# Where the causal mask is added in a segment-recurrent attention kernel: a matmul of the identity, or an add on VectorE

## The chip, the cores and the metric

The kernel runs on one core of a Trainium2 chip. The metric is the device time of one execution in microseconds (us). Engines go by their short names: PE is TensorE's matmul stream, PEld its weight loads, DVE is VectorE, ACT is ScalarE, POOL is GpSimd, SP is the engine that issues most of the DMAs. PSUM is the memory that PE writes its sums into; DVE and ACT read them from there.

## What is computed

Two pairs of layers run one after the other over a sequence of 2048 tokens of width 448. Layer A is attention with 16 heads of 256, in segments of 32 tokens; each segment attends to 8 memory rows and to itself, and its first 8 output rows are the memory of the next segment. Layer B is a gated feed-forward. The part of the reference that matters:

```
def _A_ref(x, mem0, Wq, Wk, Wv, Wo, seg_len):
    ...
    L = M + seg_len
    idx = jnp.arange(L)
    mask = (idx[:, None] < M) | (idx[:, None] >= idx[None, :])
    mem = mem0
    for s in range(n_seg):
        h = jnp.concatenate([mem, xs], axis=1)
        ...
        scores = jnp.einsum('bhqe,bhke->bhqk', q, k) * scale
        scores = jnp.where(mask[None, None], scores, -1000000000.0)
        p = _softmax(scores, axis=-1)
        ...
        mem = o[:, :M, :].copy()
...
x = x + _A_ref(_layernorm(x, axis=-1), ...)
x = x + _B_ref(_layernorm(x, axis=-1), ...)
x = x + _A_ref(_layernorm(x, axis=-1), ...)
x = x + _B_ref(_layernorm(x, axis=-1), ...)
```

## The kernel before, in words

At the start (until 93.6 us, where the first matmul of a step stands) the weights of query and key, and of value and output, are multiplied into one matrix per head pair (`A_sb`, `B_sb`). Then 69 steps follow, `for g in range(nsteps + 1)`. Step g works on segment g of the first attention layer and, four steps later, on segment g-4 of the second one; the code calls these two the chains. `active(g)` gives the chains of a step: only the first for g = 0 to 3, both for g = 4 to 63, only the second for g = 64 to 67. So there are 60 **two-layer steps**, 30 with even g and 30 with odd g. Odd steps also carry the feed-forward (`Feed`: `gate_up` and `down`), which gives PE more to do.

The 16 heads are in two halves, hf = 0 and 1 (8 heads times 16 rows are 128 partitions). In a step, in the order in which `step` issues it:

- `project` (L383) multiplies the tokens by `A_sb`, seven groups for each half; the results go from PSUM to the tiles `TQ` and `TZ`.
- `scores_m` (L458) makes the scores `Sm` of the 8 memory rows of both chains and calls `weights_of` (L412), the softmax on DVE and ACT: `mx` (L415, largest of a row), `se` (L417, subtract it), Exp on ACT (L418), `ssum` (L420), `rs` (L422, reciprocal), for the memory rows `rs` times `blk` (L424), and the product into `PM` or `PX` (L425).
- `flipped` (L427) transposes `PM` on PE into the PSUM tile `pps`, and DVE copies it to `PT` (L432).
- `scores_x` (L466) makes the scores `Sx` of the segment rows, a tile of 128 x 4 x 40 in one PSUM tile. In the kernel before, the first matmul is the identity times `maskS` (128 x 160 numbers, 0 or -1e6, built once at the start), which puts the mask there; 16 matmuls of 40 columns are then added to it.
- `weigh_m` (L479) multiplies the tokens by `PT`: two matmuls into `ya`, three into `yb`. DVE copies `ya` to `Y` (L485), ACT copies `yb` to `Y` (L490).
- `project_out` (L522) multiplies `Y` by `B_sb` into `ox`, the largest piece of PE's work; `weigh_x` and `finish` follow.

**What sets the order.** All matmuls and transposes of the steps go through `mm` (L73) and `tr` (L76), and `in_order` chains each to the one before: PE runs them exactly in the order of the program. The middle of a step is, on PE: pps of PM for half 0, Sx for half 0, ya and yb for half 0, Sm for half 1, Sx for half 1, then in odd steps three `gate_up`, then 72 matmuls of `project_out(0, 0, 18)`, then pps of PM for half 1 and of PX for half 0, 12 matmuls of ox, ya and yb for half 1. On DVE and ACT nothing of the kind is written: there the language's planner lays out the order when the kernel is built, from which instruction can run when, and with what is written earlier in the program first; each engine then runs its list strictly in that order. PSUM tiles with the tag `ps` share 7 buffers; `ox` has one of its own.

Of the kernel before, what the change touches and what calls it, by code (L numbers as in the profile page):

```python
# [9 lines left out]
F32 = mybir.dt.float32  # L10
I32 = mybir.dt.int32
AF = mybir.ActivationFunctionType
ALU = mybir.AluOpType
# [8 lines left out]
L = MEM + SEG  # L22
# [23 lines left out]
def build_kernel(ctx, tc, A_x, A_mem0, A_Wq, A_Wk, A_Wv, A_Wo, B_W_gate, B_W_up, B_W_down, out,  # L46
                 ntiles=16, nseg=64):
    nc = tc.nc
    P = nc.NUM_PARTITIONS
# [15 lines left out]
    def in_order(r):  # L65
        if last_pe[0] is not None:
            tc.add_manual_dep(r.ins, last_pe[0],
                              mybir.DependencyInfo(mybir.DependencyClass.NoSync,
                                                   mybir.DependencyReason.DATA),
                              reason="order of issue")  # L70
        last_pe[0] = r.ins.name

    def mm(*a, **k):  # L73
        in_order(nc.tensor.matmul(*a, **k))  # L74
# [19 lines left out]
    ident = glob.tile([P, P], BF, name="ident")  # L94
# [17 lines left out]
    maskS = glob.tile([P, 4, L], BF, name="maskS")  # L112
# [11 lines left out]
    half = glob.tile([P, 1], F32, name="half")  # L124
# [13 lines left out]
    with tc.tile_pool(name="pre", bufs=6) as pre:  # L138
# [35 lines left out]
        for p in range(NP):  # L174
            hf, p4 = divmod(p, 4)
# [20 lines left out]
        for p in range(NP):  # L196
            hf, p4 = divmod(p, 4)
# [4 lines left out]
            for eo in range(2):  # L202
                for kd in range(3):
                    bps = psum.tile([P, 512], F32, tag="ps", name="bps")
                    for t in range(2):
                        e = 2 * eo + t
                        nc.tensor.matmul(bps[:, 0:DM], vT[:, e, kd * 128:(kd + 1) * 128], wo[:, e, :],  # L207
                                         start=(t == 0), stop=(t == 1))
                    evac(next_eng(), B_sb[:, hf, tidx(kd, eo, p4), 0:DM], bps[:, 0:DM])
            bps = psum.tile([P, 512], F32, tag="ps", name="bps")  # L210
            for t in range(2):
                for eo in range(2):
                    e = 2 * eo + t
                    nc.tensor.matmul(bps[64 * eo:64 * eo + 64, 0:DM], vT[:, e, 384:448], wo[:, e, :],
                                     start=(t == 0), stop=(t == 1), tile_position=(0, 64 * eo))
# [18 lines left out]
    main = ctx.enter_context(tc.tile_pool(name="main", bufs=1))  # L234
# [11 lines left out]
    TQ, TZ, YB, PX, PM = [], [], [], [], []  # L246
# [129 lines left out]
    def moving(hb, j, idx, chains):  # L376

        if len(chains) == 2:
            return hb[:, j, idx * HI:(idx + 1) * HI].rearrange("p (c k) -> p c k", k=64)[:, :, 0:L]
        c = chains[0]  # L380
        return hb[:, j, idx * HI + 64 * c:idx * HI + 64 * c + L]
# [27 lines left out]
    def queries(hf, g, kd):  # L409
        return TQ[hf][:, g, 2 * kd:2 * kd + 2, :] if kd < 3 else TZ[hf][:, g, :]  # L410

    def weights_of(Sp, n, dst, keep, tag):  # L412

        mx = main.tile([P, n], F32, tag=f"mx{tag}", name="mx")
        nc.vector.tensor_reduce(mx[:], Sp[:], axis=AX.X, op=ALU.max)  # L415
        se = main.tile([P, n, L], F32, tag=f"se{tag}", name="se")
        nc.vector.tensor_tensor(se[:], Sp[:], mx[:].unsqueeze(2).to_broadcast([P, n, L]), op=ALU.subtract)  # L417
        nc.scalar.activation(se[:], se[:], AF.Exp, scale=SCALE)  # L418
        ssum = main.tile([P, n], F32, tag=f"ssum{tag}", name="ssum")
        nc.vector.tensor_reduce(ssum[:], se[:], axis=AX.X, op=ALU.add)  # L420
        rs = main.tile([P, n], F32, tag=f"rs{tag}", name="rs")
        nc.vector.reciprocal(rs[:], ssum[:])  # L422
        if keep is not None:
            nc.vector.tensor_tensor(rs[:], rs[:], keep, op=ALU.mult)  # L424
        nc.vector.tensor_tensor(dst[:, :, 0:L], se[:], rs[:].unsqueeze(2).to_broadcast([P, n, L]), op=ALU.mult)  # L425
# [9 lines left out]
    def active(g):  # L435
        return [c for c in (0, 1) if 0 <= g - c * LAG < nseg]

    def step(g, ff):
        chains = active(g)
# [18 lines left out]
        def scores_m(hf):  # L458
            if not ms:
                return  # L460
            Sp = psum.tile([P, 2, L], F32, tag="ps", name="Sm")
            for kd in range(4):
                mm(Sp[:, :, :], queries(hf, 2, kd), moving(hb, j, kd, (0, 1)), start=(kd == 0), stop=(kd == 3))
            weights_of(Sp, 2, PM[hf], blk[:], f"m{hf}")

        def scores_x(hf):  # L466
            Sp = psum.tile([P, 4, L], F32, tag="ps", name="Sx")
            mm(Sp[:, :, :], ident[:], maskS[:], start=True, stop=False, skip_group_check=True)
            for half in range(2):
                for c in chains:  # L470
                    for kd in range(4):
                        mm(Sp[:, 2 * half + c, :], queries(hf, 3 * c + half, kd), moving(hb, j, kd, (c,)),
                           start=False, stop=(half == 1 and c == chains[-1] and kd == 3), skip_group_check=True)
            return Sp

        def probs_x(hf, Sp):
            weights_of(Sp, 4, PX[hf], None, f"x{hf}")

        def weigh_m(hf, hk, PT):  # L479
            if not ms:  # L480
# [81 lines left out]
        project(1, chains, hb, j, (4, 5))  # L562
        pm = flipped(PM[0], 1, "m0")
        Sx0 = scores_x(0)
        weigh_m(0, hk, pm)
        scores_m(1)
        Sx1 = scores_x(1)
        probs_x(0, Sx0)
        feed(0, 1, 2)
        project_out(0, 0, 18)  # L570
        probs_x(1, Sx1)
        pm = flipped(PM[1], 1, "m1")
        px0 = flipped(PX[0], 2, "x0")
# [101 lines left out]
```

## Time and profile before

| what | value |
|---|---|
| time, median of 3 runs (lowest, highest) | 1735.13 us (1734.34, 1735.6) |
| the profiled execution's own time | 1736.02 us |
| its span in the profile | 1734.2 us |
| mean granted TensorE clock | 0.992 |
| POOL busy | 84.4 us (5%) |
| one even and the next odd step, by the stages view, 801.86 to 821.51 and 821.51 to 850.71 us | 19.65 and 29.20 us |
| of these, DVE busy | 12.75 and 19.75 us |

The profiled execution took 0.89 us longer than the median. The page of a profile gives the busy time of each engine and its share of the span; groups of instructions by line and tile, where `Sx<-maskS,ident` means that the tile Sx was written from maskS and ident; and a chain that ended last, followed back from the last instruction. The timeline lists instructions in order of time (start, length, engine, line, operation, tile, count); neighbours of one kind are merged into a row with a count, and a bracket at the end gives the idle time before it and what ended that. Where a length is given for a matmul, it includes its way through the array; the next matmul starts long before it ends, so PE's pace is read from the starts.

### The profile page before, as it was taken

The numbers are of one execution on the slowest core, as the hardware profiler recorded it, in microseconds if no ns is written. First come the engines' busy times: TensorE is split into PE (matmuls) and PEld (weight loads), VectorE is DVE, ScalarE is ACT, GpSimd is POOL, SyncE is SP. The second block draws the span as 40 slices with busy tenths as digits, with TensorE's granted clock in tenths as the row PEclk, the third lists the DMA queues.
The fourth block names the chain that finished last, engine by engine and source line by source line (L and its number), as shares of the span: only waits on it lengthen the run. The fifth ranks groups of instructions, "written<-read, shape, count | busy, mean of one in ns | idle before, by whom it ended". The sixth has DMA issues, their size and how long they took to land.

```text
span 1734.2 us, 90637 instructions
## 1 busy us (share of the span) xinstructions
PE 1700.2 (98%) x41498; PEld 1597.2 (92%) x41498; DVE 1139.0 (66%) x3805; ACT 668.3 (39%) x1951; POOL 84.4 (5%) x191
## 2 busy tenths in 40 slices
PE   7889999999999999999999999999999999999998
PEld 5578999999999999999999999999999999999987
DVE  6656666766666667666666666666666666666664
ACT  5633333433333343433333343333333343333332
POOL 2220000000000000000000000000000000000000
PEclk9979999999999999999999999999999999999999
DMA  8330000000000000000000000000000000000000
GB/s 242 109 114 8 8 4 8 9 9 9 9 9 8 9 4 9 9 9 8 9 9 9 7 4 9 9 9 9 9 8 9 7 5 9 9 7 6 6 6 6
DMA packets 25983, 32.65 MB, mean 19 GB/s; under 512 B 3064, under 2 KB 23936, under 8 KB 25600
## 3 DMA queue, kind: packets, MB, share of 16 engines
q1 hardware_dynamic: 24512, 23.18, 4.9%
q8 instruction: 324, 5.31, 1.3%
q0 software_dynamic: 1088, 3.68, 0.7%
q14 instruction: 59, 0.48, 0.1%
HBM read 23.18 MB, written 1.84 MB: 14 GB/s over the span
## 4 chain that ended last, share of the span: by engine, by line
PE 95%; DVE 3%; ACT 1%; issue 1%; DMA 0%; POOL 0%; SPq 0%; POOLq 0%; DVEq 0%; ACTq 0%
PE ox L74 30%; PE prj L74 30%; PE ups L74 6%; PE gps L74 6%; PE dps L74 5%; PE y L74 4%; PE Sx L74 3%; PE pps L77 1%; PE aps L186 1%; PE bps L207 1%; PE Sm L74 1%; PE ya L74 1%; PE tps L77 1%; PE yb L74 1%; PE kps L77 1%; PE tpw L169 1%
## 5 line engine op out<-in xcount | busy, mean ns | idle before, releaser
L74 PE MATMUL ox<-Y,B_sb 128*128 128x80 bf16 (+4 forms) x15456 | 590.7, 199 | 1.4 <-issue 1.4
L74 PE MATMUL prj<-hT,A_sb 128*128 128x80 bf16 (+1 forms) x15232 | 571.7, 200 | 5.4 <-DVE hT L305 3.7
L74 PEld LDWEIGHTS <-B_sb 128*128 128x128 bf16 x15456 | 564.3, 99 | 11.8 <-issue 1.8
L74 PEld LDWEIGHTS <-A_sb 128*128 128x128 bf16 x15232 | 547.2, 100 | 12.8 <-issue 5.9
L81 ACT CAST TQ<-prj 128x320 bf16<-128x320 f32 (+1 forms) x456 | 169.8, 384 | 168.6 <-PE prj L74 136.9
L83 DVE CAST TQ<-prj 128x320 bf16<-128x320 f32 (+1 forms) x456 | 192.8, 431 | 49.6 <-PE prj L74 42.3
L83 DVE CAST Y<-y 128x128 bf16<-128x128 f32 (+2 forms) x384 | 162.1, 463 | 54.8 <-PE y L74 34.3
L81 ACT CAST Y<-y 128x512 bf16<-128x512 f32 (+2 forms) x384 | 144.1, 417 | 81.2 <-PE y L74 54.8
L345 DVE SCALAR_TENSOR_TENSOR hh<-gps,ut 128x256 bf16<-128x256 f32 (+1 forms) x238 | 95.6, 402 | 100.3 <-PE gps L74 92.0
L432 DVE COPY PT<-pps 128x128 bf16<-128x128 bf16 (+1 forms) x272 | 63.7, 255 | 119.6 <-PE pps L77 113.3
L74 PE MATMUL ups<-xT,Wu_sb 128*128 128x128 bf16 (+1 forms) x1904 | 140.1, 217 | 0.5 <-DVE xT L331 0.5
L74 PE MATMUL gps<-xT,Wg_sb 128*128 128x128 bf16 (+1 forms) x1904 | 140.1, 217 | 0.0
L344 ACT CAST ut<-ups 128x256 bf16<-128x256 f32 (+1 forms) x238 | 84.3, 355 | 105.8 <-PE ups L74 101.0
L490 ACT CAST Y<-yb 128x192 bf16<-128x192 f32 x134 | 42.6, 318 | 189.4 <-PE yb L74 189.4
L74 PEld LDWEIGHTS <-Wg_sb 128*128 128x128 bf16 x1904 | 111.9, 98 | 0.0
L74 PEld LDWEIGHTS <-hk 40*128 40x128 bf16 (+1 forms) x1950 | 96.3, 96 | 16.2 <-issue 0.6
L74 PEld LDWEIGHTS <-Wu_sb 128*128 128x128 bf16 x1904 | 109.7, 98 | 0.7 <-issue 0.7
L418 ACT ACTIVATE se<-se 128x80 f32<-128x80 f32 (+1 forms) x270 | 74.6, 299 | 89.5 <-DVE se L417 87.8
L74 PE MATMUL dps<-Wd_sb,hh 128*128 128x448 bf16 x476 | 95.9, 353 | 0.0
L272 POOL TENSOR_SCALAR rstd<-mv 128x1 f32<-128x1 f32 x67 | 14.7, 220 | 1561.6 <-DVE mv L270 1561.6
L74 PEld LDWEIGHTS <-TQ 128*128 128x128 bf16 x1938 | 86.7, 97 | 0.2 <-ACT TQ L81 0.2
L81 ACT CAST TZ<-prj 64x320 bf16<-64x320 f32 (+2 forms) x152 | 56.0, 378 | 78.6 <-DVE TZ L83 77.6
(112 smaller groups left out, 1797.6 us busy)
## 6 DMA issues: line engine op xcount, KB each, us to landing
wo<-in_A_Wo_dram POOLq DMA_DIRECT2D x8, 448.0 KB, 6.0
nat<-in_A_Wq_dram SPq DMA_DIRECT2D x8, 384.0 KB, 5.5
nat<-in_A_Wk_dram SPq DMA_DIRECT2D x8, 384.0 KB, 5.6
nat<-in_A_Wv_dram SPq DMA_DIRECT2D x8, 384.0 KB, 3.8
xa<-in_A_x_dram SPq DMA_DIRECT2D x32, 56.0 KB, 2.3
xa<-xp SPq DMA_DIRECT2D x32, 56.0 KB, 1.9
out_dram<-xa SPq DMA_DIRECT2D x32, 56.0 KB, 2.0
xp<-in_A_x_dram SPq DMA_DIRECT2D x30, 56.0 KB, 2.1
```

What stands on the lines that cost most here:

```text
L74: in_order(nc.tensor.matmul(*a, **k))
L77: in_order(nc.tensor.transpose(*a))
L81: nc.scalar.copy(dst, src)
L83: eng.tensor_copy(dst, src)
L169: nc.tensor.transpose(tp[:, e, kd * 128:(kd + 1) * 128], nat[:, kd, (2 * e2 + e) * 128:(2 * e2 + e + 1) * 128], ident[:])
L186: nc.tensor.matmul(aps[:, :, :], qT[:, e, kd * 128:(kd + 1) * 128], kT[:, e, 0:384], start=(t == 0), stop=(t == 1))
L207: nc.tensor.matmul(bps[:, 0:DM], vT[:, e, kd * 128:(kd + 1) * 128], wo[:, e, :], start=(t == 0), stop=(t == 1))
L344: nc.scalar.copy(ut[:, :, n], ups[:, :, n])
L345: nc.vector.scalar_tensor_tensor(out=hh[:, 2 * u:2 * u + 2, n], in0=gps[:, :, n], scalar=0.0, in1=ut[:, :, n], op0=ALU.max, op1=ALU.mult)
L418: nc.scalar.activation(se[:], se[:], AF.Exp, scale=SCALE)
L432: nc.vector.tensor_copy(PT[:], pps[:].rearrange("p b q -> p (b q)"))
L490: nc.scalar.copy(YB[hf][:, 16:28, M0:M0 + 16], yb[:].rearrange("p (t q) -> p t q", q=16))
```

## The change

In two-layer steps the identity matmul with the mask goes. The first matmul of each group of four (kd = 0) starts its own sum instead. `weights_of` gets the mask as an argument, and DVE adds it while it reads `Sx` out of PSUM and writes the sum to the tile `se`; the row maximum and the subtraction then read `se` in SBUF, and the subtraction writes `se` in place. One-layer steps and the memory scores keep their form.

```diff
-    def weights_of(Sp, n, dst, keep, tag):
+    def weights_of(Sp, n, dst, keep, tag, mask=None):
 
         mx = main.tile([P, n], F32, tag=f"mx{tag}", name="mx")
+        se = main.tile([P, n, L], F32, tag=f"se{tag}", name="se")
+        if mask is not None:
+            nc.vector.tensor_tensor(se[:], Sp[:], mask, op=ALU.add)
+            Sp = se
         nc.vector.tensor_reduce(mx[:], Sp[:], axis=AX.X, op=ALU.max)
-        se = main.tile([P, n, L], F32, tag=f"se{tag}", name="se")
         nc.vector.tensor_tensor(se[:], Sp[:], mx[:].unsqueeze(2).to_broadcast([P, n, L]), op=ALU.subtract)
...
         def scores_x(hf):
             Sp = psum.tile([P, 4, L], F32, tag="ps", name="Sx")
-            mm(Sp[:, :, :], ident[:], maskS[:], start=True, stop=False, skip_group_check=True)
+            both = len(chains) == 2
+            if not both:
+                mm(Sp[:, :, :], ident[:], maskS[:], start=True, stop=False, skip_group_check=True)
             for half in range(2):
                 for c in chains:
                     for kd in range(4):
                         mm(Sp[:, 2 * half + c, :], queries(hf, 3 * c + half, kd), moving(hb, j, kd, (c,)),
-                           start=False, stop=(half == 1 and c == chains[-1] and kd == 3), skip_group_check=True)
+                           start=(both and kd == 0), stop=(kd == 3), skip_group_check=True)
             return Sp
 
         def probs_x(hf, Sp):
-            weights_of(Sp, 4, PX[hf], None, f"x{hf}")
+            weights_of(Sp, 4, PX[hf], None, f"x{hf}", maskS[:] if len(chains) == 2 else None)
```

## The prediction, made before the result was known

> **What bounds the kernel now.** I read the page first, then the groups by shape, then the timeline of PE and of DVE through one even and one odd step.
>
> ```profile
> PE 1700.2 (98%) x41498; PEld 1597.2 (92%) x41498; DVE 1139.0 (66%) x3805; ACT 668.3 (39%) x1951; POOL 84.4 (5%) x191
> ...
> PE 95%; DVE 3%; ACT 1%; issue 1%; DMA 0%; POOL 0%; SPq 0%; POOLq 0%; DVEq 0%; ACTq 0%
> ```
>
> PE holds 95% of the chain that ended last, and its order is fixed by the code: a matmul that disappears is worth its slot, unless PE then waits for somebody at the next place. The row of the disappearing group:
>
> ```profile
> L74 PE MATMUL Sx<-maskS,ident 128*128 128x160 bf16 x136 | 32.0, 235 | 0.0
> ```
>
> 235 ns is its length through the array, not its price; the price is the distance to the next start. PE in an even step in the middle of the span:
>
> ```profile
> 810.19 0.22 PE L77 MATMUL pps<-ident,PM 128*128 128x128 bf16 x1
> 810.25 0.23 PE L74 MATMUL Sx<-maskS,ident 128*128 128x160 bf16 x1
> 810.32 0.23 PE L74 MATMUL Sx<-hT,TQ 128*128 128x40 bf16 x3
> ...
> 810.70 0.18 PE L74 MATMUL Sx<-hT,TZ 128*128 128x40 bf16 x1
> 810.73 0.27 PE L74 MATMUL ya<-PT,hk 128*128 128x128 bf16 x2
> ...
> 811.09 0.23 PE L74 MATMUL Sx<-maskS,ident 128*128 128x160 bf16 x1
> ...
> 811.54 0.18 PE L74 MATMUL Sx<-hT,TZ 128*128 128x40 bf16 x1
> 811.62 0.45 PE L74 MATMUL ox<-Y,B_sb 128*128 128x80 bf16 x8
> ```
>
> The mask's slots are 0.07 us each (in the trace's nanoseconds 69 in half 0, 72 in half 1, the same in every steady step). See also the two joints: Sx to ya takes 31 ns and Sx to ox 81 ns, where Sx to ups, the odd step's next matmul, takes 25. DVE beside it:
>
> ```profile
> 810.45 0.23 DVE L432 COPY PT<-pps 128x128 bf16<-128x128 bf16 x1
> 810.91 0.33 DVE L415 TENSOR_REDUCE mx<-Sx 128x4 f32<-128x160 f32 x1 [0.24 <-PE Sx L74]
> 811.15 0.41 DVE L485 CAST Y<-ya 128x256 bf16<-128x256 f32 x1
> 811.49 0.23 DVE L415 TENSOR_REDUCE mx<-Sm 128x2 f32<-128x80 f32 x1
> 811.63 0.31 DVE L417 TENSOR_TENSOR se<-Sx,mx 128x160 f32<-128x160 f32 x1
> ...
> 813.74 0.23 DVE L425 TENSOR_TENSOR PM<-se,rs 128x80 bf16<-128x80 f32 x1
> 813.89 0.17 DVE L422 RECIPROCAL rs<-ssum 128x4 f32<-128x4 f32 x1
> 814.10 0.33 DVE L425 TENSOR_TENSOR PX<-se,rs 128x160 bf16<-128x160 f32 x1
> 814.46 0.42 DVE L432 COPY PT<-pps 128x128 bf16<-128x128 bf16 x2
> ```
>
> DVE is 66% busy over the span, but from 810.9 to 814.9 it has hardly a gap: here an added DVE instruction has no cover. In odd steps the two PT copies come at 837.18, after 1.67 us of idle DVE.
>
> **Two gates that already hold.** In each of the 54 two-layer steps between 250 and 1590 us, ya of half 0 starts 53 to 55 ns after the copy PT ends, and in each of the 27 even ones ox starts 53 to 54 ns after Y<-ya ends. A distance so fixed is a wait with its signal's latency; where the profile names such a wait (pps for PM, at 183.60 us), it is 54 to 60 ns too. So (1) ya, in even and odd steps, is held by PT, and (2) ox, in even steps, by Y<-ya. PE hides it almost whole: 31 instead of 25 ns, 81 instead of 25.
>
> **The change part by part.**
>
> *Mask, half 0: 60 slots of 69 ns go, gain nil.* From pps to ya runs 259 ns to the copy's start, 225 of copying, 54 of signal: 538 ns, and none of it is touched. PE does Sx 69 ns sooner and waits those 69 ns in front of ya. Only a fall of the gate would return them (60 x 0.069 = 4.1 us); the lower end, nothing, is what the rows say.
>
> *Mask, half 1, odd steps: 30 x 0.072 = 2.2 us gained.* Next is ups, which waits for nothing (25 ns). DVE's extra work there ends before the 1.67 us idle.
>
> *Mask, half 1, even steps: set by Y<-ya.* Y now starts at 811.153 because `mx` of Sx holds DVE (240 ns from start to next start); ya itself would let it start 315 ns after ya, as it does for half 1, at 811.044. After: the add takes mx's place, starts 69 ns sooner (810.844) and holds DVE for 231 ns, taken from `se<-Sx,mx` (also two inputs, 160 numbers, from PSUM: 811.633 to 811.864). Then Y at 811.075, ox 78 ns sooner: 30 x 0.078 = 2.3 us. The add itself isn't in the trace: between 210 ns (811.812 to 812.022, the shortest of that kind) and 336 (mx at 812.012, which ran into a wait) ox gains 96 ns (then ACT's copy of yb, which ends 150 ns before ox, holds it) or loses 27: -2.9 to +0.8 us over 30. I take the nearest row. The start flags and the tile made earlier add no instruction, and Sx's PSUM buffer is free sooner than before, after the add instead of after se.
>
> That the planner puts Y next, not mx, I read from the list above: Y, mx of Sm, se of Sx follow program order whenever their input is there, and the new mx, waiting for the add's result (end + 0.04 as in mx 808.10+0.24 to se 808.38), can't be ready before 811.19.
>
> *DVE: two adds in each two-layer step, 120 in all, 120 x 0.231 = 28 us of DVE work.* mx and se read SBUF instead of PSUM: I take no difference, since PX<-se,rs (SBUF) takes 312 ns and se<-Sx,mx (PSUM) 309. In odd steps idle DVE hides all 14 us. In even steps the deadlines are: PM 54 ns before pps (now 218, so 164 ns of slack), PX the same (now 856: 0.8 us), and PT for half 1, whose ya comes 115 ns after it instead of 54: 61 ns of slack, counted from pps. If everything on DVE from 811.1 on moved by 0.46 us, that would cost 0.3 us a step. But the memory scores come first in the program, so the adds go into their gaps. Laid out by hand with the start-to-start distances above (0.23 for 160 numbers, 0.15 for 80, 0.08 for the small ones): add x0 810.84, Y 811.08, mx m 811.42, mx x0 811.57, se m 811.80, se x0 811.95, add x1 812.18, ssum m 812.41, mx x1 812.55, rs m 812.78, ssum x0 812.86, rs*blk 813.09, se x1 813.17, PM 813.40, rs x0 813.55, PX x0 813.75, ssum x1 813.98, rs x1 814.34, PT m 814.42, PX x1 after it. The same rules give the list of before in its real order. PE is at pps at 814.12 (ox at 811.54 + 2.574): PM, done 813.63, is early; PX, done 814.06, is just in time; PT could start at 814.38, starts at 814.42, within its 61 ns. No new wait, but by hundredths: I cost it at 0 and keep 0 to +0.31 us a step (0 to +9.4 us) for the range.
>
> [...]
>
> *Sum:* 0 - 2.2 - 2.3 + 0 = -4.5; the first and last two-layer steps are narrower, so -4.4. From the profiled execution's 1736.02 that is 1731.6; from the median of 1735.13, 1730.7 us (-0.25%).
>
> **The rivals.**
>
> R1, *a late tail on DVE in even steps* (the other sign): PX x1 stands before PT m in DVE's list, since it is earlier in the program. If it became ready at 814.52 as in my list, PT would start at 814.75 and end at 814.98; ya at 815.03 instead of 814.72: +0.31 x 30 = 9.4, net +5.0, 1740.1. It decides from 0.15 us a step on (4.5/30). PX x0 or PM late by a tenth or two gives the same kind of wait at pps, net -3 to +2. For: DVE has no gap here. Against: the hand list.
>
> R2, *mx before Y* in DVE's list: Y at 811.43, ox at 811.90 instead of 811.62; 30 x 0.28 = 8.3, less the odd 2.2: +6.1, 1741.2. Against: the readiness above, by 0.11 us.
>
> R3, *both slots come back*: 60 x (0.069 + 0.072) = 8.5: 1726.7. Against: the 53 to 55 ns.
>
> R4, *the work moves and nothing else*: the even steps' gain is eaten by small waits; -2.2 and about: 1733.
>
> **How the numbers follow.** Forecast 0.40, R4 0.22, R1 0.20, R2 0.12, R3 0.06. A measurement of this kernel tells some 0.2%, 3.5 us, from no change. Faster: forecast but for its weak edge (0.36) and R3 (0.06): 0.42. Slower: R2 and most of R1 beyond 3.5 (0.15): 0.27. Same: the rest, 0.31. The forecast's own range is 1729.5 to 1732; over the cases it is 1729 to 1741, which leaves out R3 and the upper half of R2.
>
> **What would show it.** Right: Sx to ya in half 0 grows from 31 to about 100 ns and PT-to-ya stays 54; the odd step is 0.07 shorter, the even one too; add, Y, mx on DVE in that order. Wrong: a bracket at pps or ya in even steps naming PM, PX or PT (R1), mx between add and Y (R2), ya sooner after pps than 0.54 (R3).

## The result, and the profile after

The changed kernel takes 1741.76 us (median of 6 runs, 1740.82 to 1742.6) where the kernel before takes 1734.38 (6 runs, 1733.56 to 1735.6): ratio 1.0039, 95% interval 1.0029 to 1.005 (the ratio is estimated from the runs and is not the plain quotient of the medians, 1.0043). By the medians it is slower by 7.4 us, by the interval 5.0 to 8.7; the forecast was 4.4 us faster, with a range up to 1741.0 us.

First the page of the changed kernel: busy time by engine, and the shares of the chain that ended last.

```profile
PE 1700.7 (98%) x41378; PEld 1594.4 (92%) x41378; DVE 1170.7 (67%) x3925; ACT 674.7 (39%) x1951; POOL 84.6 (5%) x191
...
PE 87%; DVE 9%; ACT 2%; issue 1%; DMA 1%; SPq 0%; POOL 0%; POOLq 0%; DVEq 0%; ACTq 0%
```

120 matmuls fewer, 120 DVE instructions more, as the diff says. PE's busy share has not moved, 98% in both (matmuls overlap, and their lengths fill small gaps: in the first rows of PE's timeline below one of 0.22 us starts at 811.69, the next at 811.75), so it says nothing here. The chain does: 8 points of it have gone from PE to DVE and ACT. That shows where to look, not how much was lost, since 8% of the span would be far more than 7 us. The groups by shape (of the changed kernel) show the parts:

```profile
L417 DVE TENSOR_TENSOR se<-Sx,maskS 128x160 f32<-128x160 f32 x120 | 38.4, 320 | 10.3 <-PE Sx L74 10.3
L420 DVE TENSOR_TENSOR se<-se,mx 128x160 f32<-128x160 f32 x120 | 37.3, 311 | 0.0
L419 DVE TENSOR_REDUCE mx<-se 128x4 f32<-128x160 f32 x120 | 36.9, 308 | 0.0
L74 PE MATMUL Sx<-maskS,ident 128*128 128x160 bf16 x16 | 3.7, 233 | 0.0
```

Now an even step, the timeline of PE in the changed kernel (start, length, engine, line, operation; the bracket is idle time before and what ended it). The steps stand elsewhere in time than before; only distances are compared.

```profile
811.69 0.22 PE L77 MATMUL pps<-ident,PM 128*128 128x128 bf16 x1
811.75 0.23 PE L74 MATMUL Sx<-hT,TQ 128*128 128x40 bf16 x3
...
812.13 0.18 PE L74 MATMUL Sx<-hT,TZ 128*128 128x40 bf16 x1
812.23 0.27 PE L74 MATMUL ya<-PT,hk 128*128 128x128 bf16 x2
```

From pps to ya it is 0.54 us, as before, though the mask's slot between them is gone: ya waits 99 ns after the last Sx instead of 31. Then the place where the time is lost, further on in the same step:

```profile
815.63 0.22 PE L77 MATMUL pps<-ident,PM 128*128 128x128 bf16 x1
815.69 0.27 PE L77 MATMUL pps<-ident,PX 128*128 128x128 bf16 x2
815.80 0.59 PE L74 MATMUL ox<-Y,B_sb 128*128 128x80 bf16 x12
816.61 0.27 PE L74 MATMUL ya<-PT,hk 128*128 128x128 bf16 x2 [0.22 <-DVE PT L435]
```

ya of half 1 comes 0.98 us after pps, and the bracket names PT. In the kernel before, the same place was:

```profile
814.20 0.22 PE L77 MATMUL pps<-ident,PM 128*128 128x128 bf16 x1
814.25 0.28 PE L77 MATMUL pps<-ident,PX 128*128 128x128 bf16 x2
814.37 0.59 PE L74 MATMUL ox<-Y,B_sb 128*128 128x80 bf16 x12
814.79 0.28 PE L74 MATMUL ya<-PT,hk 128*128 128x128 bf16 x2
```

There it was 0.60 us (598 ns), without a bracket. DVE of the changed kernel beside it:

```profile
812.35 0.32 DVE L417 TENSOR_TENSOR se<-Sx,maskS 128x160 f32<-128x160 f32 x1 [0.17 <-PE Sx L74]
812.59 0.41 DVE L490 CAST Y<-ya 128x256 bf16<-128x256 f32 x1
812.92 0.23 DVE L419 TENSOR_REDUCE mx<-Sm 128x2 f32<-128x80 f32 x1
813.07 0.31 DVE L419 TENSOR_REDUCE mx<-se 128x4 f32<-128x160 f32 x1
...
814.47 0.30 DVE L419 TENSOR_REDUCE mx<-se 128x4 f32<-128x160 f32 x1
...
815.05 0.23 DVE L428 TENSOR_TENSOR PM<-se,rs 128x80 bf16<-128x80 f32 x1
815.20 0.32 DVE L428 TENSOR_TENSOR PX<-se,rs 128x160 bf16<-128x160 f32 x1
815.53 0.32 DVE L423 TENSOR_REDUCE ssum<-se 128x4 f32<-128x160 f32 x1
815.89 0.18 DVE L425 RECIPROCAL rs<-ssum 128x4 f32<-128x4 f32 x1
816.10 0.32 DVE L428 TENSOR_TENSOR PX<-se,rs 128x160 bf16<-128x160 f32 x1
816.34 0.41 DVE L435 COPY PT<-pps 128x128 bf16<-128x128 bf16 x2
```

PT could start 0.26 us after pps, at 815.89. It starts at 816.34, since ssum, rs and PX of half 1 stand before it in DVE's list; DVE even stands idle 34 to 35 ns (in the trace's nanoseconds) before rs and before PX, because each needs the one before. This is the prediction's rival R1, in its place, and the bracket that names PT is the sign that the prediction gave for it. PX of half 1 stood ahead of PT in the kernel before, too (814.10 and 814.46 in the prediction's lines), but there it held nobody up: the order of these two is the old one, and what the adds did is to make PX later.

In nanoseconds, medians over the steady two-layer steps between 250 and 1590 us (26 to 28 of each kind in each profile; the single values differ by some 10 ns at most):

| | before | after |
|---|---|---|
| even step | 20102 | 20412 |
| odd step | 28755 | 28687 |
| half 0: last Sx to ya | 31 | 99 |
| half 0: end of PT to ya | 54 | 53 |
| even: ya to Y's start | 427 | 360 |
| even: end of Y to ox | 54 | 53 |
| even, half 1: pps to PT's start | 259 | 717 |
| even, half 1: pps to ya | 598 | 985 |

30 x 310 - 30 x 68 ns are 7.3 us: the whole difference of the medians, 7.4, with its place.

### The profile page after: what moved, and what is told of

It reads as the page before. It is cut to its first block, busy times and chain, and to the rows that moved or that the text cites. A ratio compares the mean times of both kernels' runs of the same rounds, so it can differ in the third digit from the quotient of the medians.

```text
span 1740.0 us, 90488 instructions
## 1 busy us (share of the span) xinstructions
PE 1700.7 (98%) x41378; PEld 1594.4 (92%) x41378; DVE 1170.7 (67%) x3925; ACT 674.7 (39%) x1951; POOL 84.6 (5%) x191
## 3 DMA queue, kind: packets, MB, share of 16 engines
q0 software_dynamic: 1088, 3.68, 0.7%
## 4 chain that ended last, share of the span: by engine, by line
PE 87%; DVE 9%; ACT 2%; issue 1%; DMA 1%; SPq 0%; POOL 0%; POOLq 0%; DVEq 0%; ACTq 0%
PE prj L74 30%; PE ox L74 25%; PE ups L74 6%; PE gps L74 6%; PE dps L74 5%; PE y L74 4%; PE Sx L74 2%; DVE ssum L423 1%; ACT se L421 1%; DVE mx L419 1%; PE pps L77 1%; PE bps L207 1%; PE ya L74 1%; DVE PX L428 1%; PE tps L77 1%; PE kps L77 1%
## 5 line engine op out<-in xcount | busy, mean ns | idle before, releaser
L74 PEld LDWEIGHTS <-B_sb 128*128 128x128 bf16 x15456 | 564.2, 99 | 11.4 <-issue 1.3
L74 PEld LDWEIGHTS <-hk 40*128 40x128 bf16 (+1 forms) x1950 | 101.6, 95 | 26.0 <-issue 9.9
L421 ACT ACTIVATE se<-se 128x80 f32<-128x80 f32 (+1 forms) x270 | 80.0, 303 | 103.8 <-DVE se L420 102.2
L81 ACT COPY hT<-tps 128x256 bf16<-128x256 bf16 x32 | 11.9, 372 | 187.4 <-DVE hT L83 187.4
```

What stands on the lines that cost most here:

```text
L81: nc.scalar.copy(dst, src)
```

## The experiments

Theory 1 is R1 with the numbers of the trace: the adds cost nothing but the delay of PT for half 1 in even steps, and that only because PX of half 1 stands ahead of it in DVE's list. Theory 2: DVE has too much to do there, each add costs, wherever it stands. Ratios are against the kernel before on the same chip, with 95% intervals; steps are medians from the profile, as above, in us.

**e1_pin: the late tail put last.** The changed kernel, with `probs_x(1, Sx1)` written behind the two `flipped` and the reciprocal tied behind the last PT copy in DVE's order:

```diff
         r = nc.vector.reciprocal(rs[:], ssum[:])
+        if behind is not None:
+            tc.add_manual_dep(r.ins, behind,
+                              mybir.DependencyInfo(mybir.DependencyClass.NoSync,
+                                                   mybir.DependencyReason.DATA),
+                              reason="behind PT")
...
-        probs_x(1, Sx1)
         pm = flipped(PM[1], 1, "m1")
         px0 = flipped(PX[0], 2, "x0")
+        probs_x(1, Sx1)
```

> After, with one thing changed: on VectorE the reciprocal of the second half's segment scores (and so PX of half 1) stands behind the two PT copies instead of ahead of them; no instruction is added. Theory 1 (late tail: PT for half 1 is late in even steps only because PX of half 1 stands before it in VectorE's list): the wait of ya for PT goes, pps to ya is 0.60 us again; even step 20.03 us (before 20.10, after 20.41), odd 28.69; 30 x 0.070 + 30 x 0.068 = 4.1 us less than before, ratio 0.9976. Theory 2 (VectorE has too much to do there, so two adds cost about 0.46 us a step wherever they stand): another instruction is late instead, the even step stays at 20.3 us or more, ratio 1.002 or more.

Measured: 1729.87 us, ratio 0.9966 (0.9954 to 0.9979); even step 20.032, odd 28.687; pps to ya 598 ns. DVE in an even step of e1_pin:

```profile
809.90 0.32 DVE L425 TENSOR_REDUCE ssum<-se 128x4 f32<-128x160 f32 x1
810.25 0.42 DVE L442 COPY PT<-pps 128x128 bf16<-128x128 bf16 x2
810.59 0.17 DVE L427 RECIPROCAL rs<-ssum 128x4 f32<-128x4 f32 x1
810.79 0.32 DVE L435 TENSOR_TENSOR PX<-se,rs 128x160 bf16<-128x160 f32 x1
```

PE beside it:

```profile
809.99 0.22 PE L77 MATMUL pps<-ident,PM 128*128 128x128 bf16 x1
810.05 0.28 PE L77 MATMUL pps<-ident,PX 128*128 128x128 bf16 x2
810.16 0.59 PE L74 MATMUL ox<-Y,B_sb 128*128 128x80 bf16 x12
810.59 0.28 PE L74 MATMUL ya<-PT,hk 128*128 128x128 bf16 x2
```

The same instructions in another order: PT starts 0.26 us after pps, the wait is gone, nothing else is late. Theory 2 falls: the load is unchanged. The even step comes out 70 ns below that of the kernel before, where the forecast had 78.

**e2_before_pin: the same order without the change.** The same edit on the kernel before.

> Before, with the same order as in e1_pin: the reciprocal and PX of half 1 behind the PT copies. Theory 1: PT of half 1 was on time already (61 ns of slack), nothing changes: even 20.10, odd 28.755, ratio 1.000. If the order of VectorE's tail is worth something by itself, the even step gets shorter here too, and the gain of e1_pin is not that of the change.

Measured: 1734.87 us, ratio 0.9997 (0.9988 to 1.0006); even step 20.101, odd 28.756. The order alone is worth nothing; it matters once the adds have made the tail late.

**e6_add_and_matmul: the cost without the gain.** `if not both:` ahead of the mask's matmul goes, so that it is always issued, and the 16 matmuls add to it as before; DVE adds the mask once more.

> The add on VectorE is there in two-layer steps, but the matmul with the mask stays too, so the mask is added twice (-2e6 instead of -1e6); this is the cost of the adds without any gain on TensorE. Theory 1: PT of half 1 as late as in after, 0.39 us; even step 20.41 + 0.07 = 20.48, odd 28.755; 30 x 0.38 = 11.4 us more than before, ratio 1.0066. If instead the loss came from the four sums that start by themselves on TensorE, even steps are 20.10 and the ratio 1.000.

Measured: 1746.6 us, ratio 1.0063 (1.005 to 1.0075); even step 20.484, odd 28.757. Against the changed kernel, e6 is slower by 72 ns in even steps and 70 in odd ones, the slot of the one matmul that nothing hides; so the four separate sums of the changed kernel cost PE nothing that shows. In odd steps the two adds cost 2 ns, less than single steps differ.

**e3_odd_only: the change in odd steps.**

```diff
-            both = len(chains) == 2
+            both = len(chains) == 2 and g % 2 == 1
...
-            weights_of(Sp, 4, PX[hf], None, f"x{hf}", maskS[:] if len(chains) == 2 else None)
+            weights_of(Sp, 4, PX[hf], None, f"x{hf}", maskS[:] if len(chains) == 2 and g % 2 == 1 else None)
```

> The change made in odd steps only; even steps keep the matmul with the mask. Both theories: even step 20.10, odd 28.69, 30 x 0.068 = 2.0 us less than before, ratio 0.9988. If the odd steps' gain is given back in the even step that follows, the ratio is 1.000.

Measured: 1733.17 us, ratio 0.9989 (0.998 to 0.9998); even step 20.102, odd 28.688. The odd steps' gain is real and is not given back.

**e4_half1 and e5_half0: one half each.** As e3_odd_only, with `hf == 1` or `hf == 0` in place of `g % 2 == 1`.

> Only half 1 of the two-layer steps gets its mask from VectorE; half 0 keeps the matmul. Theory 1, laid out by hand from the times of before: the add takes the place of mx of half 1, and mx, se, ssum and the rest of that half each come one place later, so PX of half 1 starts about 0.6 us later than before and PT for half 1 0.48 us late, 0.42 after its slack; ox gains nothing in even steps, since Y still waits for mx of half 0. Even step 20.5 us, odd 28.69; 30 x 0.42 - 30 x 0.068 = 10.4 us more than before, ratio 1.006. Theory 2 (the load counts, each add alike): half of what the two adds cost, even step 20.25 or so, ratio 1.001.

Measured: 1744.27 us, ratio 1.0051 (1.0037 to 1.0065); even step 20.490, odd 28.687; PT starts 720 ns after pps.

> Only half 0 of the two-layer steps gets its mask from VectorE; half 1 keeps the matmul. Theory 1: on TensorE the slot of half 0 is worth nothing in odd steps (ya waits for PT; odd step 28.755); in even steps Y starts 67 ns sooner and ox with it, at most 56; by hand PT for half 1 is 0.22 us late, 0.16 after its slack: even step 20.20 to 20.27, 3 to 5 us more than before, ratio 1.002 to 1.003. If the slot of half 0 were worth its 69 ns on TensorE, the odd step would be 28.69.

Measured: 1735.27 us, ratio 1.0002 (0.9993 to 1.0011); even step 20.142, odd 28.756; PT starts 428 ns after pps, ya 101 ns later than before; ox starts 25 ns after the last Sx. The wait was smaller than expected (101 ns, not 160), and so the step missed the 20.20 to 20.27 and the time the 3 to 5 us; the kind of wait is as expected. The add of half 1 alone makes PT as late as both adds together (720 and 717 ns): it lies in that half's own chain. With the add of half 0 on top, even steps are 78 ns shorter, not longer, since Y starts sooner.

Here is what puts the tail of e4_half1 so late; DVE in an even step of it:

```profile
816.55 0.32 DVE L420 TENSOR_TENSOR se<-se,mx 128x160 f32<-128x160 f32 x1
816.79 0.23 DVE L428 TENSOR_TENSOR PM<-se,rs 128x80 bf16<-128x80 f32 x1
817.27 0.32 DVE L423 TENSOR_REDUCE ssum<-se 128x4 f32<-128x160 f32 x1 [0.25 <-ACT se L421]
817.63 0.18 DVE L425 RECIPROCAL rs<-ssum 128x4 f32<-128x4 f32 x1
817.84 0.33 DVE L428 TENSOR_TENSOR PX<-se,rs 128x160 bf16<-128x160 f32 x1
818.08 0.41 DVE L435 COPY PT<-pps 128x128 bf16<-128x128 bf16 x2
```

DVE stands idle 0.25 us for Exp on ACT, and PX starts only when rs has ended, with PT behind both. In this kernel it is a chain's length, not a lack of DVE time.

**e7_half1_pin and e8_half0_pin: one half each, tail last.** The two edits joined.

> As e4_half1 (mask from VectorE in half 1 only), with the reciprocal and PX of half 1 behind the PT copies as in e1_pin. Theory 1 (an add costs only through PT of half 1): the 0.39 us a step of e4_half1 vanish whole; even step 20.10, since ox still waits for Y there, odd 28.687: 30 x 0.068 = 2.0 us less than before, ratio 0.9988. Theory 2 (load): even step stays above 20.3, ratio above 1.002.

Measured: 1731.67 us, ratio 0.9982 (0.9974 to 0.9991); even step 20.101, odd 28.686.

> As e5_half0 (mask from VectorE in half 0 only), with the same pin. Theory 1: the even step loses the 0.10 us that PT cost there and keeps the 0.056 that ox gains by an earlier Y: 20.045; odd 28.755, as the slot of half 0 is worth nothing there. 30 x 0.057 = 1.7 us less than before, ratio 0.9990. With e7_half1_pin this parts the 4.1 us of e1_pin: 2.0 from odd steps by half 1 alone; in even steps half 0's earlier Y and half 1's slot are needed together.

Measured: 1732.62 us, ratio 0.9983 (0.9974 to 0.9992); even step 20.043, odd 28.757. With PT in front, an add costs nothing that shows in any step. And the slot of half 1 is worth nothing in even steps as long as Y waits for mx of half 0: half 1 alone makes none of the 70 ns, half 0 alone 58.

**e9_pin_early: the first gate lifted.** e1_pin, with the transpose of PM for half 0 issued four matmuls earlier, inside the last projection group:

```diff
             for p4 in range(4):
+                if p4 == 3 and u == us[-1] and inside is not None:
+                    inside()
                 for kd in range(4):
...
-        project(1, chains, hb, j, (4, 5))
-        pm = flipped(PM[0], 1, "m0")
+        early = []
+        project(1, chains, hb, j, (4, 5), lambda: early.append(flipped(PM[0], 1, "m0")))
+        pm = early[0]
```

> As e1_pin, and on TensorE the transpose pps of PM for half 0 stands four matmuls earlier, inside the last projection group, so that PT is ready 0.14 us sooner; no instruction is added. Theory 1 (ya of half 0 waits for PT, which is why the first slot is worth nothing): the wait goes, last Sx to ya is 25 to 31 ns again; odd steps get the second slot too, 28.62; in even steps Y starts when the add lets VectorE go, so ox gains nothing more: 20.03. 30 x 0.07 + 30 x 0.136 = 6.2 us less than before, ratio 0.9964. If the wait had another cause, ya stays 99 ns behind and the times are those of e1_pin.

Measured: 1728.5 us, ratio 0.9964 (0.9952 to 0.9977); even step 20.033 as expected, odd 28.659, not 28.62. PE in an odd step of e9_pin_early:

```profile
826.87 0.18 PE L74 MATMUL Sx<-hT,TZ 128*128 128x40 bf16 x1
826.89 0.27 PE L74 MATMUL ya<-PT,hk 128*128 128x128 bf16 x2
...
827.12 0.32 PE L74 MATMUL Sm<-hT,TQ 128*128 128x80 bf16 x3
```

and ACT there:

```profile
826.75 0.42 ACT L81 CAST TQ<-prj 128x320 bf16<-128x320 f32 x1 [1.00 <-PE prj L74]
```

ya now follows Sx without a wait (PT ended 122 ns before it), so the first gate was what the prediction took it for. But the third matmul of Sm, which needs this copy of TQ, starts 56 ns after it ends (827.227 after 827.171), and 55 to 57 ns in all 27 odd steps. It starts 74 ns after the second one, where 35 is the rule in e1_pin: a next gate, not seen before, holds PE for 39 ns, and of the 69 ns the step gains 28. This is the fastest version of the study by its median; the intervals don't part it from e1_pin.

**e10_before_early: the same without the change.**

> Before, with the transpose pps of PM for half 0 four matmuls earlier as in e9_pin_early. Theory 1: there the wait for PT was only 6 ns, so odd steps 28.75 and even ones 20.10, ratio 1.000. If the earlier transpose is worth something by itself, it shows here without the change.

Measured: 1735.19 us, ratio 1.0002 (0.9993 to 1.0011); even step 20.102, odd 28.748. Lifting that gate alone is worth 7 ns in odd steps, the 6 ns that PE had waited.

## Why the prediction was wrong, step by step

- *Mask of half 0: nil.* Right: pps to ya stays 536 to 538 ns, and the wait grows to 99; R3, by which this slot would come back, did not happen. e9_pin_early shows that PT is the cause: with PT sooner, ya comes sooner (826.89, behind the last Sx at 826.87).
- *Mask of half 1, odd steps: 30 x 72 ns.* Right: 68 ns each (28755 to 28687), alone in e3_odd_only and e7_half1_pin too.
- *Even steps, set by Y.* Right in order (add, Y, mx, so not R2) and nearly in size: Y starts 67 ns sooner, 78 were said; the add, 323 to 325 ns long, held DVE for 240 to 242 ns, like mx, not for 231. (The row of 210 ns that the prediction puts at 811.812 to 812.022 stands at 812.812 to 813.022 in the trace.) The gain is lost again in the same step, and shows as 70 ns in e1_pin.
- *No gap from SBUF or PSUM.* Right: mx from SBUF takes 308 ns (319 before, from PSUM), se 311 (309).
- *DVE's deadlines: "PT could start at 814.38, starts at 814.42, within its 61 ns. No new wait", with PX x1 after it.* **This step failed.** The list by hand had PT ready at 814.38 and PX of half 1 ready at 814.52, and let the first to be ready go first. The built list has PX first, and DVE ran it in that order (PT could start at 815.89, but DVE stood idle for 35 ns, to 816.10, and then took PX): PT starts 458 ns later than it could (717 to 259), ya 387 later than it did, against 310 in R1. The hand list was nearly right in its times: from the add of half 0 to PX of half 1 it had 3.68 us, the trace has 3.75. It had other orders wrong too (in the trace, ssum of half 0 goes before mx of half 1, for one), but the order that cost was that of PT and PX of half 1, 0.14 us apart in the list, and such a tie was priced as a small risk: 0.20 for R1, of which 0.05 was counted as within the noise. The built list of the kernel before already had PX in front; the forecast needed the planner to swap the two.
- *The sum:* 7.3 us for -4.5. The failed step is 30 x 0.380 = 11.4 us of it (even steps of the changed kernel against those of e1_pin); without it, the steps of e1_pin give -4.1, and the interval of its ratio is 3.6 to 8.0 us faster. The range missed by 0.8 us because R1's term was mis-sized: 0.387 us of wait instead of 0.31, 2.3 us over 30 steps, which is about the 0.07 us by which PX came later than in the hand list.

What stays open: why the planner puts PX of half 1 first. R1's reason, that it stands earlier in the program, is not it: written behind the `flipped` but without the tie, it stands in the same place of the built list (that version was not timed), so the tie was needed. No run shows by what the planner goes.

## What to carry to other kernels

Here work moved from a full engine (PE, 98% busy) to one that is a third idle (DVE, 66% before and 67% after) was free only where each instruction behind it in that engine's own list had slack: odd steps became 68 ns shorter, even ones 310 ns longer (PT of half 1 came 458 ns later there). So look at the busy stretch, not at the share, and at which instruction of the critical engine waits behind the lengthened chain. When a list that a planner makes decides between two instructions a tenth of a microsecond apart (0.14 us here), treat the order as unknown, price both, or fix it by hand. And before a removed instruction is counted, look whether its successor starts a fixed distance after something else: then the slot was a cover for that wait (here 69 ns of slot in half 0, and ya 53 to 55 ns after PT with it or without).

## What the runs showed of the hardware

- A matmul that waited for what DVE or ACT wrote started 52 to 59 ns after that instruction ended, in each of the gates: PT to ya 52 to 55, Y to ox 52 to 54, TQ to Sm 55 to 57 (in e9_pin_early), and PM to pps 57 to 59 in the eleven places of each profile, before and after, where a bracket names that wait. Such a constant is how a wait is found that the profile's idle times don't name: the row of ya in the kernel before, at 810.73, has no bracket.
- In the two-layer steps between 250 and 1590 us, before and after, a DVE instruction that reads 160 numbers in each partition lasted 292 to 328 ns. One behind it that did not need its result started, in all pairs but one, 66 to 88 ns before its end, 209 to 249 ns after its start (add 812.35, Y 812.59 in the changed kernel); one that needed it, next in the list, started 34 to 35 ns after its end (rs ends at 816.066, PX starts at 816.101). So the chain of ssum, rs and PX of half 1 left DVE idle twice in each even step of the changed kernel, for 34 to 35 ns, and PT, which could have started at 815.89, did not use the second gap, as it stood behind PX in the list.
- Before the change, an even step repeated within 5 ns (27 steps) and an odd one within 6 (26 steps), after it within 9 and 5. So a difference of 70 ns in 30 of the steps, 0.1% of the time in all, can be read from one profile, where the times of the whole kernel just tell it from nothing (e3_odd_only: 0.998 to 0.9998).
